# Block means by short products with the values standing, one load for the first value rows, and load costs by run length, in an attention and two-layer kernel

## The chip, the cores and the metric

The kernel runs on one core of a Trainium2 chip. The metric is the device time of one execution in microseconds (us). An execution is timed as a whole; the profile shows the span from the first to the last instruction on the core, which is a little shorter.

## What is computed

Local attention with block summaries, then two gated feed-forward stages, all in 32-bit floats:

```python
# B, H, S, D = 2, 8, 768, 64; block 32, window 16, nb = 24 blocks
k_sum = k.reshape(B, H, nb, block, D).max(axis=3)
v_sum = v.reshape(B, H, nb, block, D).mean(axis=3)
scores_l = scale * (q @ k.T), masked to |i - j| < window
scores_s = scale * (q @ k_sum.T) + log(block)
a = softmax over [scores_l, scores_s]
x = a @ concat([v, v_sum])              # 1536 tokens x 512
x = (silu(x @ w_gate) * (x @ w_val)) @ w_out        # 512 -> 1536 -> 512
out = (h * tanh(softplus(h))) @ w_out2, h = x @ w_in2   # 512 -> 2048 -> 512
```

## The kernel before

Attention is cut into 24 units: batch b, a third tb of the tokens (256), and a pair p of heads, in the order b, tb, p. A unit loads its queries (`loads`, 128 KB, runs of 1 KB in memory) and its windows of values (`load_v`, 192 KB into `vext[p]`: 96 rows, four windows, 128 columns, so runs of 512 bytes). `scores` makes the products of queries and keys (line 420), the scaled and masked scores with their minimum on VectorE (line 441), the exponentials on ScalarE (458) and the normalisation (483 on VectorE or 493 on ScalarE). `transposes` turns the weights (507) and copies them back; `values` makes the products with the values (523); its result is split into a high and a low part, `xh` by a copy on ScalarE (line 268) and `xl` by a subtraction on VectorE (line 282).

Each row of `vext[p]` below the 96 window rows holds the 24 block means. For the first batch they are made by `means_first`: six loads of 256 KB, six products on TensorE (line 342) in which a constant matrix of 128x120 stands and a tile of 128 tokens x 512 columns moves, summed in one bank, and then four copies on ScalarE into `vext[p]`. For the second batch `means_second` does the same when unit 6 is set up: six loads into `pacc`, six such products into one bank, one copy of 24x512 to `vsm`, from where `do_vext` spreads them by DMA.

The feed-forward stages work with numbers split in two fp32r parts, three products for one. Weights come as 512 KB tiles of 4 KB runs into four `raw` slots; each is put together by `words32` (lines 627 on ScalarE, 634, 643 and 652 on VectorE) and split into `wsl` (268 on ScalarE, 282 on VectorE). The first products that use them are those of `hidden` (line 722); the later stages are lines 773, 822 and 1005.

The order of the work is made by a planner in the program itself (`Program.order`). Every step is registered with an engine, a cost in ns, what it reads and writes, and for some a time at which it is wanted; the planner then lets the engines run by these costs and at each moment gives an engine, among the steps that are ready, the one whose latest allowed start is earliest. What comes out is a fixed order for each engine, which the chip follows whether or not its times are those of the planner. The transfers are all on the queue of SyncE. Their cost is `c_dma`; a transfer starts when the ones ahead have used up the planner's DMA time, and lands 1750 ns after its own share. `FIRST_LOADS` names the transfers that go first, in this order. Where TensorE has nothing to do by the planner's times, ahead of the first product of line 773, the planner puts filling products on a constant tile (line 256), in number 0.8 times the gap over 430 ns, and four at the start.

Of the kernel before, what the change touches and what calls it, by code (L numbers as in the profile page):

```python
# [17 lines left out]
P = 128  # L18
B, H, S, D = 2, 8, 768, 64
BLOCK, WINDOW = 32, 16  # L20
NB = S // BLOCK
SP = WINDOW + S + WINDOW
TQ = 64
NTILE = S // TQ
WIN = TQ + 2 * WINDOW
KC = WIN + NB
CCOLS = 3 * KC + P + KC + NB - P // BLOCK
NPAIR = H // 2
NT = B * S
DM = H * D  # L30
# [23 lines left out]
NORM_I, NORM_J = 4, 16  # L54


FIRST_LOADS = "k0 q0 c k1 q1 k2 q2 k3 q3 m0 m1 m2 m3 m4 m5 w0 w1 t0 w2 t1 w3 t2".split()

FILL_FIRST, FILL = 4, 0.8
EARLY, MEANS, NQ = 40e3, 25e3, 4  # L60
# [125 lines left out]
    return 100 + 2.35 * n  # L186


def c_dma(nbytes):
    return nbytes / 290.0  # L190


@with_exitstack
def tile_kernel(
# [14 lines left out]
    nc = tc.nc  # L209
# [7 lines left out]
    cst = sb.tile([P, CCOLS], F32, name="cst")  # L217
# [21 lines left out]
        for p in range(NPAIR)  # L239
    ]  # L240
    vx, qq = att[0:KC, 2 * KX :], att[:, 2 * KX + NPAIR * 512 :]
    vext = [vx[:, p * 512 : (p + 1) * 512].rearrange("p (n d) -> p n d", d=P) for p in range(NPAIR)]
    qraw = [qq[:, i * HALF : (i + 1) * HALF] for i in range(NQ)]
    qc = [
        qq[:, (NQ + i) * HALF : (NQ + i + 1) * HALF].rearrange("p (n q) -> p n q", q=TQ) for i in range(3)
# [7 lines left out]
    op = pg.add  # L253
# [3 lines left out]
    SC, PT, T1 = (0, 1, 2), (3, 4), (5, 6, 7)  # L257


    def dma(dst, src, nbytes, r=(), w=(), name=None, **more):  # L260
        if name in FIRST_LOADS:
            more["want"] = (FIRST_LOADS.index(name) - 100) * 500.0
        op("SP", c_dma(nbytes), lambda: nc.sync.dma_start(out=dst, in_=src), r=r, w=w, **more)

    def copy(dst, src, n, psum, r, w, scale=1.0, eng="ACT"):

# [23 lines left out]
    def att_bank(i):  # L290
        banks_used["n"] += 1
        ring = (2, 3, 6, 7, 4, 5) if i < 4 else (2, 3, 6, 7)
        return ring[banks_used["n"] % len(ring)]

    def do_k(b, p):
        ke, key = kext[p], ("kext", p)
        src = kt[b, p]
        if b == 0:

            stage = pacc[p // 2].rearrange("p m f -> p (m f)")[:, (p % 2) * 1024 : (p % 2) * 1024 + SP]  # L300
            sk = [("pacc", p // 2, m) for m in (2 * (p % 2), 2 * (p % 2) + 1)]
            dma(stage, src, P * SP * 4, w=sk, name=f"k{p}")
            win = bass.AP(stage.tensor, stage.offset, [stage.ap[0], [TQ, NTILE], [1, WIN]])
            copy(ke[:, :, 0:WIN], win, NTILE * WIN, False, sk, [key], eng=KE[p])
        else:
            win = bass.AP(src.tensor, src.offset, [[SP, P], [TQ, NTILE], [1, WIN]])
            dma(ke[:, :, 0:WIN], win, P * NTILE * WIN * 8, w=[key])
        ks = ksm[p % 2]
        op(
            "DVE",  # L310
            c_dve(S),
            lambda: nc.vector.tensor_reduce(
                out=ks.rearrange("p (t n) -> p t n", n=TQ // BLOCK),
                in_=ke[:, :, WINDOW : WINDOW + TQ].rearrange("p t (n r) -> p t n r", r=BLOCK),
                axis=AX.X,
                op=ALU.max,
            ),
            r=[key],
            w=[("ksm", p % 2)],
        )  # L320
        copy(
            ke[:, :, WIN:KC],
            ks.unsqueeze(1).to_broadcast([P, NTILE, NB]),
            NTILE * NB,
            False,
            [("ksm", p % 2)],
            [key],
            eng="POOL" if b else "DVE",
        )

    def means(b, bufs, bk):

        nt = S // P
        for t in range(nt):
            buf, key = bufs[t % len(bufs)]
            src = vt[b, WINDOW + t * P : WINDOW + (t + 1) * P, :]
            dma(buf, src, P * 2048, w=[key], name=f"m{b * nt + t}", rel=b * MEANS)
            at = NB - P // BLOCK - t * (P // BLOCK)
            op(
                "PE",  # L340
                860,
                lambda t=t, at=at, buf=buf: nc.tensor.matmul(  # L342
                    bank[bk][0:KC, :], mean[:, at : at + KC], buf, start=(t == 0), stop=(t == nt - 1)
                ),
                r=[key, "cst"],
                w=[("bank", bk)],
            )
# [21 lines left out]
    vsm, kvsm = pacc[1][WIN:KC, 3, :], ("pacc", 1, 3)  # L369

    def means_second():
        bk = att_bank(NPAIR)
        means(1, [(pacc[m // 4][:, m % 4, :], ("pacc", m // 4, m % 4)) for m in range(7)], bk)
        copy(vsm, bank[bk][WIN:KC, :], 512, True, [("bank", bk)], [kvsm])

    def do_vext(p):
        dma(
# [7 lines left out]
    def loads(i):  # L385
        b, tb, p = units[i]
        raw_q = qraw[i % NQ]
        dma(raw_q, qt[b, tb, p].rearrange("j d q -> (j d) q"), P * 1024, w=[("qraw", i % NQ)], name=f"q{i}")
        copy(
            qc[i % 3],  # L390
            raw_q.rearrange("d (q n) -> d n q", n=4),
            HALF,
            False,
            [("qraw", i % NQ)],
            [("qc", i % 3)],
            eng=QE[i] if i < NPAIR else "POOL",
        )

    def load_v(i):
        b, tb, p = units[i]  # L400
        src = vt[b, tb * HALF :, p * P : (p + 1) * P]
        win = bass.AP(src.tensor, src.offset, [[DM, WIN], [TQ * DM, 4], [1, P]])
        dma(vext[p][0:WIN, :, :], win, WIN * 2048, w=[("vext", p)], name=f"w{i}")

    def scores(i):

# [702 lines left out]
```

## Time and profile before

| | us |
|---|---|
| median of 3 runs | 630.26 (629.48 to 630.62) |
| the profiled execution | 629.81 |
| its span on the core | 627.8 |
| TensorE busy in the span | 616.9 |
| VectorE busy | 443.5 |
| ScalarE busy | 300.9 |
| GpSimd busy | 16.3 |

The span and the busy times come from the profiled execution; 2.0 us of its time lie outside the span. Busy time of TensorE is a union of its products' durations and does not say that each of them was at full rate, nor that each was needed: the filling products count too. The attention units run from 0 to some 125 us, overlapped with the first feed-forward stage from 26 us on.

### The profile page before, as it was taken

To read this page: it belongs to the slowest core of one execution; us is meant where nothing else is said; L and a number is where in the kernel's file an instruction comes from. 1 tells how busy PE (TensorE), PEld (TensorE's weight loads), DVE (VectorE), ACT (ScalarE), POOL (GpSimd) and SP (SyncE) were. 2 spreads that over 40 slices of the span, in tenths; PEclk is the share of its full clock that TensorE was granted. 3 is DMA by queue.
4 is the path that set the end of the run, shared out by engine and by line. 5 is a ranking of instruction groups with operands and counts; after the bars stand their busy time and mean duration, and the time that the engine had idled before them with its cause. 6 is when DMAs were issued, how large, how long until landed. Compare 5 with 4: busy or idle time off the path is not lost.

```text
span 627.8 us, 10576 instructions
## 1 busy us (share of the span) xinstructions
PE 616.9 (98%) x4020; PEld 530.6 (85%) x4020; DVE 443.5 (71%) x1075; ACT 300.9 (48%) x700; POOL 16.3 (3%) x29
## 2 busy tenths in 40 slices
PE   8999999999999999999999999999999999999997
PEld 5668989888888888888888888898989898989895
DVE  6898679665843884662665999689738985896553
ACT  5889998643512451331332545555443643362321
POOL 0021211000000000000000000000000000000000
PEclk9999999999999999999999999999999999999999
DMA  9985684012400350030200121213300340010111
GB/s 291 341 219 142 172 277 149 14 68 68 138 30 2 130 171 1 22 113 1 67 1 1 68 101 34 68 68 98 104 1 20 116 134 1 15 54 1 67 68 67
DMA packets 33713, 54.99 MB, mean 88 GB/s; under 512 B 8576, under 2 KB 21248, under 8 KB 33664
## 3 DMA queue, kind: packets, MB, share of 16 engines
q1 hardware_dynamic: 33664, 54.33, 27.9%
q8 instruction: 31, 0.51, 0.4%
q14 instruction: 18, 0.15, 0.1%
HBM read 50.98 MB, written 3.15 MB: 86 GB/s over the span
## 4 chain that ended last, share of the span: by engine, by line
PE 90%; ACT 4%; DMA 2%; DVE 2%; issue 1%; DVEq 0%; ACTq 0%; SPq 0%
PE bank L822 33%; PE bank L722 30%; PE bank L1005 19%; PE bank L773 3%; PE bank L420 2%; PE bank L523 2%; PE bank L507 1%; DMA raw<-in_w_val_dram 1%; ACT att_tmp L458 1%; PE bank L342 1%; ACT att_tmp L493 1%; DMA raw<-in_w_out_dram 1%; ACT cvs L627 1%; PE bank L256 1%; ACT att_tmp L268 1%
## 5 line engine op out<-in xcount | busy, mean ns | idle before, releaser
L722 PE MATMUL bank<-xh,wsl 128*128 128x512 f32 (+1 forms) x672 | 203.9, 363 | 0.9 <-DVE tmps L972 0.4
L722 PEld LDWEIGHTS bank<-xh,wsl 128*128 128x128 f32 x672 | 123.7, 188 | 22.4 <-DVE tmps L962 1.5
L822 PE MATMUL bank<-wsl,gt 128*128 128x512 f32 x576 | 135.5, 390 | 0.0
L822 PEld LDWEIGHTS bank<-wsl,gt 128*128 128x128 f32 x576 | 106.5, 188 | 21.0
L722 PE MATMUL bank<-xl,wsl 128*128 128x512 f32 (+1 forms) x336 | 120.4, 358 | 0.0
L822 PE MATMUL bank<-gt,wsl 128*128 128x512 f32 x360 | 91.3, 389 | 0.0
L1005 PE MATMUL bank<-xh,wsl 128*128 128x256 f32 x384 | 80.7, 283 | 1.1 <-ACT tmps L268 1.1
L822 PEld LDWEIGHTS bank<-gt,wsl 128*128 128x128 f32 x360 | 67.4, 188 | 13.9
L282 DVE TENSOR_TENSOR tmps<-tmps,bank 128x256 f32<-128x256 f32 x132 | 53.0, 416 | 33.9 <-PE bank L1005 31.9
L268 ACT ACTIVATE wsl<-cva 128x512 fp32r<-128x512 f32 (+1 forms) x84 | 50.5, 608 | 50.0 <-DVE cva L652 20.5
L722 PEld LDWEIGHTS bank<-xl,wsl 128*128 128x128 f32 x336 | 63.3, 188 | 9.4 <-issue 0.2
L962 DVE SCALAR_TENSOR_TENSOR tmps<-tmps,bank 128x512 f32<-128x512 f32 (+1 forms) x42 | 25.3, 603 | 61.8 <-ACT tmps L955 61.7
L1005 PEld LDWEIGHTS bank<-xh,wsl 128*128 128x128 f32 x384 | 64.9, 191 | 2.3 <-ACT tmps L268 1.3
L282 DVE TENSOR_TENSOR gt<-tmps,gt 128x512 fp32r<-128x512 f32 (+1 forms) x78 | 50.2, 645 | 21.7 <-ACT gt L268 17.4
L268 ACT ACTIVATE gt<-tmps 128x512 fp32r<-128x512 f32 (+1 forms) x77 | 45.4, 593 | 40.4 <-DVE tmps L972 39.1
L955 ACT ACTIVATE tmps<-bank 128x512 f32<-128x512 f32 (+1 forms) x42 | 22.5, 535 | 85.6 <-PE bank L722 85.5
L282 DVE TENSOR_TENSOR wsl<-cva,wsl 128x512 fp32r<-128x512 f32 (+1 forms) x84 | 55.1, 661 | 6.0 <-ACT wsl L268 6.0
L1005 PE MATMUL bank<-xl,wsl 128*128 128x256 f32 x192 | 54.3, 283 | 0.0
L1005 PE MATMUL bank<-att_late,wsl 128*128 128x256 f32 x320 | 49.3, 283 | 0.0
L627 ACT ACTIVATE cvs<-raw 128x512 f32<-128x512 f32 x68 | 44.8, 666 | 8.5 <-DVE cva L652 7.7
L652 DVE SCALAR_TENSOR_TENSOR cva<-cvs,cva 128x512 uint32<-128x512 uint32 x68 | 47.0, 692 | 0.5
L643 DVE SCALAR_TENSOR_TENSOR cva<-cvs,cva 128x512 uint32<-128x512 uint32 x68 | 46.0, 684 | 1.8 <-ACT cvs L627 0.6
(83 smaller groups left out, 687.2 us busy)
## 6 DMA issues: line engine op xcount, KB each, us to landing
raw<-in_w_out_dram SPq DMA_DIRECT2D x28, 512.0 KB, 3.7
raw<-in_w_in_dram SPq DMA_DIRECT2D x16, 512.0 KB, 3.6
raw<-in_w_gate_dram SPq DMA_DIRECT2D x12, 512.0 KB, 4.3
raw<-in_w_val_dram SPq DMA_DIRECT2D x12, 512.0 KB, 3.7
att<-in_vt_dram SPq DMA_DIRECT2D x24, 192.0 KB, 4.5
att<-in_qt_dram SPq DMA_DIRECT2D x24, 128.0 KB, 3.4
out_dram<-pacc SPq DMA_DIRECT2D x8, 256.0 KB, 2.1
pacc<-in_kt_dram SPq DMA_DIRECT2D x4, 400.0 KB, 6.0
```

What stands on the lines that cost most here:

```text
L268: cost, fn = c_act(n, psum), lambda: nc.scalar.activation(out=dst, in_=src, func=AF.Copy, scale=scale)
L282: op(eng, c_dve(n), lambda: nc.vector.tensor_tensor(out=dst, in0=a, in1=b, op=alu), r=r, w=w)
L420: nc.tensor.matmul(parts_[2 * j + n // 2][q, :], qb[d, n, :], ke[d, 4 * tb + n, :], start=True, stop=True)
L627: lambda: nc.scalar.activation(out=f32(q), in_=f32(high), func=AF.Copy, scale=2.0**-112),
L643: lambda: nc.vector.scalar_tensor_tensor(out=a, in0=q, scalar=3, in1=a, op0=ALU.logical_shift_left, op1=ALU.bitwise_or),
L652: lambda: nc.vector.scalar_tensor_tensor(out=a, in0=q, scalar=0x80000000, in1=a, op0=ALU.bitwise_and, op1=ALU.bitwise_or),
L722: nc.tensor.matmul(ps, a, x, start=(kk == 0 and m == 0), stop=(kk == KD - 1 and m == 2))
L773: nc.tensor.matmul(bank[bk][:, col : col + HALF], w[:, a, mm], gg[:, x, 0:sz], start=(n in starts and both == 1 and q == 0 and m % 2 == 0) ...
L822: nc.tensor.matmul(bank[m], lhs, rhs, start=(n in starts and both == 1 and q == 0), stop=(n in ends and both == 0),)
L955: lambda: nc.scalar.activation(out=t, in_=gate, func=AF.Tanh, scale=0.5),
L962: lambda: nc.vector.scalar_tensor_tensor(out=t, in0=t, scalar=1.0, in1=gate, op0=ALU.add, op1=ALU.mult),
L1005: nc.tensor.matmul(bank[bk][:, 0:HALF], w, x()[:, kk, :], start=(kk == 0 and m == 0), stop=(kk == 1 and m == 2),)
```

## The change

Three edits. The means of the second batch are made with the value tile standing and four constant columns moving: 24 products of 128x128 by 128x4 in place of six of 128x120 by 128x512, whose results (128 x 96) are copied by ScalarE into a tile that GpSimd has set to zero, turned back by four transposes on TensorE, and copied to `vsm` as before. The value windows of units 0 to 3 come in one load of 96 rows x 4 windows x 2 KB in place of four loads with runs of 512 bytes; for this `vext` is laid out window by window, so that the four pairs lie side by side. And the planner's cost of a load goes by the length of its runs: 390 bytes a ns from 2 KB, 300 from 1 KB, 215 below, in place of 290 for all; the key windows of the second batch are also counted at 4 bytes a number in place of 8.

```diff
-FIRST_LOADS = "k0 q0 c k1 q1 k2 q2 k3 q3 m0 m1 m2 m3 m4 m5 w0 w1 t0 w2 t1 w3 t2".split()
+FIRST_LOADS = "k0 q0 c k1 q1 k2 q2 k3 q3 m0 m1 m2 m3 m4 m5 w0 t0 t1 t2".split()
-def c_dma(nbytes):
-    return nbytes / 290.0
+def c_dma(nbytes, run=4096):
+    return nbytes / (390.0 if run >= 2048 else 300.0 if run >= 1024 else 215.0)
-    vext = [vx[:, p * 512 : (p + 1) * 512].rearrange("p (n d) -> p n d", d=P) for p in range(NPAIR)]
+    vext = [vx[:, 0:2048].rearrange("k (n p d) -> k p n d", p=NPAIR, d=P)[:, p] for p in range(NPAIR)]
-            dma(ke[:, :, 0:WIN], win, P * NTILE * WIN * 8, w=[key])
+            dma(ke[:, :, 0:WIN], win, P * NTILE * WIN * 4, w=[key], run=4 * WIN)
     def means_second():
-        bk = att_bank(NPAIR)
-        means(1, [(pacc[m // 4][:, m % 4, :], ("pacc", m // 4, m % 4)) for m in range(7)], bk)
-        copy(vsm, bank[bk][WIN:KC, :], 512, True, [("bank", bk)], [kvsm])
+        nt, nb = S // P, P // BLOCK
+        bk, bt = att_bank(NPAIR), att_bank(NPAIR)
+        sums = pacc[1][:, 2, 0 : NPAIR * KC].rearrange("p (a c) -> p a c", c=KC)
+        ks = ("pacc", 1, 2)
+        op("POOL", 300, lambda: nc.gpsimd.memset(pacc[1][:, 2, 0 : NPAIR * KC], 0.0), w=[ks])
+        blocks = mean[:, KC - nb : KC]
+        for t in range(nt):
+            buf, key = pacc[t // 4][:, t % 4, :], ("pacc", t // 4, t % 4)
+            src = vt[1, WINDOW + t * P : WINDOW + (t + 1) * P, :]
+            dma(buf, src, P * 2048, w=[key], rel=MEANS)
+            def products(t=t, buf=buf):
+                for p in range(NPAIR):
+                    at = p * NB + t * nb
+                    nc.tensor.matmul(
+                        bank[bk][:, at : at + nb], buf[:, p * P : (p + 1) * P], blocks, start=True, stop=True
+                    )
+            op("PE", 480, products, r=[key, "cst"], w=[("bank", bk)])
+        copy(
+            sums[:, :, WIN:KC],
+            bank[bk][:, 0 : NPAIR * NB].rearrange("p (a c) -> p a c", c=NB),
+            NPAIR * NB, True, [("bank", bk)], [ks],
+        )
+        def turn():
+            for p in range(NPAIR):
+                nc.tensor.transpose(bank[bt][0:KC, p * P : (p + 1) * P], sums[:, p, :], ident)
+        op("PE", 4 * 109, turn, r=[ks, "cst"], w=[("bank", bt)])
+        copy(vsm, bank[bt][WIN:KC, :], 512, True, [("bank", bt)], [kvsm])
     def loads(i):
-        dma(raw_q, ..., P * 1024, w=[("qraw", i % NQ)], name=f"q{i}")
+        dma(raw_q, ..., P * 1024, w=[("qraw", i % NQ)], name=f"q{i}", run=1024)
     def load_v(i):
         b, tb, p = units[i]
+        if i < NPAIR:
+            if i == 0:
+                win = bass.AP(vt.tensor, vt.offset, [[DM, WIN], [TQ * DM, 4], [1, DM]])
+                dst = vx[0:WIN, 0:2048].rearrange("k (n d) -> k n d", d=DM)
+                dma(dst, win, WIN * 8192, w=[("vext", h) for h in range(NPAIR)], name="w0")
+            return
-        dma(vext[p][0:WIN, :, :], win, WIN * 2048, w=[("vext", p)], name=f"w{i}")
+        dma(vext[p][0:WIN, :, :], win, WIN * 2048, w=[("vext", p)], run=512)
```

## Rows read from the trace of the kernel before

**Rows 1.** The page, busy time and share of the span by engine.
```profile
PE 616.9 (98%) x4020; PEld 530.6 (85%) x4020; DVE 443.5 (71%) x1075; ACT 300.9 (48%) x700; POOL 16.3 (3%) x29
```
**Rows 2.** Busy us in stretches of 10 us; then granted clock, DMA share, GB/s.
```profile
20.00:30.00 10.00, 8.62 (x101) 6.46 (x101) 8.90 (x30) 8.76 (x25) 1.48 (x2) 1.00 1.05 362
30.00:40.00 10.00, 9.65 (x70) 5.82 (x66) 9.38 (x30) 8.14 (x25) 1.77 (x2) 1.00 1.10 295
40.00:50.00 10.00, 9.46 (x117) 8.14 (x116) 9.89 (x37) 9.57 (x31) 2.39 (x3) 1.00 0.55 149
50.00:60.00 10.00, 9.55 (x123) 8.71 (x122) 7.96 (x31) 9.80 (x39) 1.61 (x3) 1.00 0.50 128
```
**Rows 3.** DMA, 10 to 24 us in 40 slices of 0.35 us: GB/s.
```profile
GB/s 392 404 421 392 386 421 380 394 366 348 214 212 200 195 274 236 168 262 316 312 319 249 211 258 260 288 265 345 294 225 237 269 259 306 307 389 389 416 395 348
```
**Rows 4.** The chain that ended last: start us, us, what.
```profile
12.01 2.58 PE bank L342 x6
15.36 2.78 PE bank L342 x6
...
20.49 0.39 ACT xh L268
20.87 0.57 ACT cvs L627
...
48.40 1.25 ACT att_tmp L493 x4
...
51.46 0.69 PE bank L523 x16
...
54.23 0.44 PE bank L507 x4
...
56.20 0.61 PE bank L523 x16
...
397.63 5.03 PE bank L1005 x42
```
**Rows 5.** VectorE in order of time: start us, us; in brackets idle before it.
```profile
17.48 0.17 DVE L471 TENSOR_SCALAR st<-st 128x4 f32<-128x4 f32 x1 [1.08 <-ACT att_tmp L458]
...
18.92 0.43 DVE L634 TENSOR_SCALAR cva<-raw 128x512 uint32<-128x512 uint32 x1 [0.17 <-DMA raw<-in_w_gate_dram]
20.91 0.42 DVE L282 TENSOR_TENSOR xl<-bank,xh 128x256 fp32r<-128x256 f32 x1 [1.56 <-ACT xh L268]
21.47 0.69 DVE L643 SCALAR_TENSOR_TENSOR cva<-cvs,cva 128x512 uint32<-128x512 uint32 x1
...
28.09 0.41 DVE L634 TENSOR_SCALAR cva<-raw 128x512 uint32<-128x512 uint32 x1
```
**Rows 6.** SyncE's issues; landing of the one at 11.09, then of all to 60 us.
```profile
11.09 0.35 SPq L263 DMA_DIRECT2D raw<-in_w_gate_dram  x1
...
14.10 0.35 SPq L263 DMA_DIRECT2D raw<-in_w_out_dram  x1
...
DMA to landing us min/median/max: 7.8/7.8/7.8
...
DMA to landing us min/median/max: 2.3/6.2/9.6
```
**Rows 7.** TensorE in order of time, the second batch's means begin.
```profile
30.37 1.98 PE L342 MATMUL bank<-pacc,cst 128*120 128x512 f32 x4
```
**Rows 8.** Groups by line: count | busy us, mean ns of one | idle before them.
```profile
L342 PEld LDWEIGHTS bank<-pacc,cst 128*120 128x120 f32 x12 | 2.0, 182 | 1.7 <-issue 1.6
L523 PEld LDWEIGHTS bank<-att_tmp,att 120*64 120x64 f32 x384 | 13.1, 137 | 6.2 <-ACT att_tmp L268 2.6 <-ACT att L268 0.9 <-ACT att_tmp L458 0.4
L268 ACT ACTIVATE att_tmp<-bank 120x512 f32<-120x512 f32 x24 | 14.1, 589 | 3.9 <-PE bank L507 3.9
L268 ACT ACTIVATE xh<-bank 128x256 fp32r<-128x256 f32 x24 | 9.0, 373 | 2.1 <-PE bank L523 1.8
L255 POOL MEMSET warm<- 128x256 f32 x1 | 0.3, 312 | 0.3 <-POOLq L1097 0.3
```

More of the change, by code (lines that the diff above doesn't have):

```diff
@@ L257, in tile_kernel, with dma @@
     SC, PT, T1 = (0, 1, 2), (3, 4), (5, 6, 7)
-    def dma(dst, src, nbytes, r=(), w=(), name=None, **more):
+    def dma(dst, src, nbytes, r=(), w=(), name=None, run=4096, **more):
         if name in FIRST_LOADS:
             more["want"] = (FIRST_LOADS.index(name) - 100) * 500.0
-        op("SP", c_dma(nbytes), lambda: nc.sync.dma_start(out=dst, in_=src), r=r, w=w, **more)
+        op("SP", c_dma(nbytes, run), lambda: nc.sync.dma_start(out=dst, in_=src), r=r, w=w, **more)
     def copy(dst, src, n, psum, r, w, scale=1.0, eng="ACT"):
@@ L371, in means_second @@
     def means_second():
-        bk = att_bank(NPAIR)
-        means(1, [(pacc[m // 4][:, m % 4, :], ("pacc", m // 4, m % 4)) for m in range(7)], bk)
-        copy(vsm, bank[bk][WIN:KC, :], 512, True, [("bank", bk)], [kvsm])
+        nt, nb = S // P, P // BLOCK
[18 more added lines that the diff above has]
+            bank[bk][:, 0 : NPAIR * NB].rearrange("p (a c) -> p a c", c=NB),
+            NPAIR * NB,
+            True,
+            [("bank", bk)],
+            [ks],
+        )
[4 more added lines that the diff above has]
+        copy(vsm, bank[bt][WIN:KC, :], 512, True, [("bank", bt)], [kvsm])
     def do_vext(p):
@@ L387, in loads @@
         raw_q = qraw[i % NQ]
-        dma(raw_q, qt[b, tb, p].rearrange("j d q -> (j d) q"), P * 1024, w=[("qraw", i % NQ)], name=f"q{i}")
+        dma(raw_q, qt[b, tb, p].rearrange("j d q -> (j d) q"), P * 1024, w=[("qraw", i % NQ)], name=f"q{i}", run=1024)
         copy(
```

## The prediction

> **What bounds the kernel now.** I read four views, each to answer the question that the one before left. The busy shares come first: TensorE is busy 98% of the span [rows 1], so whatever does not change what TensorE does late in the kernel has to show up as TensorE starting its dense part earlier or doing less in it. The stretches of 10 us come second: between 20 and 50 us TensorE is not the only full engine; VectorE is busy 28.2 of 30 us there (8.90, 9.38, 9.89) and ScalarE 26.5 [rows 2]. All three edits bear on the first 50 us, so the question is who is late there. The chain of waits is third: it runs over TensorE until 18.14 us (the first batch's means end there, 15.36 + 2.78), then over ScalarE's copies and conversions, VectorE's conversions of weights, ScalarE's normalisations and exponentials, and only from 51.46 us over TensorE without a break [rows 4]. The second batch's means begin at 30.37 us [rows 7], inside the part in which the chain is not on TensorE. VectorE's own timeline is fourth: it stands idle 1.08 us before 17.48, 0.17 before 18.92 and 1.56 before 20.91, 2.8 us in all [rows 5], and from 20.91 on it has hardly a gap until 50. So the start is a stream of conversions and softmax steps on VectorE and ScalarE, fed by loads; what makes this stream begin sooner moves the whole rest of the kernel, and what only relieves TensorE before 51 us need not.
>
> **Part 1, the first value rows as one load.** The loads from 10 us on run at 348 to 421 GB/s (390 on average) until 13.5 us, then at 168 to 345 for 25 slices of 0.35 us, and after 22.2 us again at 348 to 416 [rows 3]. The slow part is the stretch in which the value loads of 512-byte runs are mixed with the first weights. Its 25 slices add up to 6481, which over 0.35 us each is 2.27 MB; at 390 GB/s these take 5.8 us and not 8.75. So the load saves at most 2.9 us of DMA time, if its 2 KB runs go as fast as the 2 KB runs of the means' loads before 13.5 us, and nothing if they do not. The Trainium skill ("DMA: Bandwidth & Descriptors", Specifications) gives 512 bytes as the size from which a transfer runs at line rate; by that rule 512-byte runs lose nothing, and this edit would be worth 0 and not 2.9 us. The slices disagree with it here.
>
> What does the saved DMA time buy? The first weight tile is issued at 11.09 and lands 7.8 us later at 18.89; VectorE takes it at 18.92 [rows 5, 6]. It now stands behind all four windows (786 KB) where it stood behind two (393 KB). At 390 GB/s the former take 2.0 us; at 215, the slow slices, the latter take 1.8; so this tile lands about when it did. The second and the third gain the most, up to 2.9 us; but the third, issued at 14.10 [rows 6], is taken by VectorE only at 28.09 [rows 5], 14 us later, while no load of the first 60 us took longer than 9.6 to land [rows 6]. So the loads are not what VectorE waits for after 20.91; the order is. That brings in part 3. The values of unit 0 now wait for the whole of the windows, not for a quarter: three quarters more, 590 KB, are 1.5 us at 390 GB/s. These windows are issued at about 10 us, ahead of the weight tile of 11.09, so they land ahead of its 18.89, while the values of unit 0 cannot start before the means' copies that follow 18.14. This cover is some 1 us deep; without it, the late part would fall on the values one for one. Three issues less on SyncE are off every path.
>
> **Part 2, the second batch's means.** Removed are six products, each two records of 0.43 us (2.58 over 6 [rows 4]): 12 x 0.43 = 5.2 us of TensorE. Added are 24 products of two records, each with a new standing tile of 128 columns and four moving columns, so 48 records. No row has this form. The lowest bound is the values' product, 0.61 us for 16 records or 0.038 us, with only 64 standing columns and halves of the array in parallel [rows 4]: 48 of them are 1.8 us. The highest is the record of line 1005 with a new 128-column tile each time, 5.03 over 42 = 0.120 us [rows 4]: 5.8 us. The transposes that come on top are four at 0.44 us together [rows 4]. The loads of standing tiles take 182 ns at 120 columns and 137 at 64 [rows 8], 45 ns for 56 columns, or 0.80 ns a column; if the loads can't overlap each other, 128 columns hold the array 0.103 us and 48 are 4.9 us. I take this, since it is the row nearest in kind: 4.9 + 0.44 = 5.4 against 5.2 us, no saving. The ends are a saving of 3.0 us (5.2 less 1.8 and 0.44) and a loss of 1.0 us (5.8 + 0.44 less 5.2). The Trainium skill ("TensorE: Matmul & The Clock Gate", LDWEIGHTS) gives a load as the columns over 1.2 in ns, whatever the rows; that is 107 ns here, an estimate of 5.1 us for the 48 and 5.6 with the transposes, and speaks against this edit as a saving. Where the planner has the work done is before 51.46 us, so each of these ends is first of all idle time of TensorE and is cut by the chain on VectorE and ScalarE. In 30 to 40 us TensorE is busy 9.65 of 10 us [rows 2], so not all of it is hidden; I put a tenth of the saving's end on the path, -0.3 us, and keep -2 and +0.5 for the range.
>
> On ScalarE a copy of 96 columns is added. Copies of 512 and 256 columns take 0.589 and 0.373 us [rows 8], 0.84 ns a column, so 96 take 0.24 us. ScalarE is busy 9.57 of 10 us in 40 to 50 us and on the chain there [rows 2, 4]: I count it in full, +0.24 us; behind it in ScalarE's order wait exponentials and weight copies. The zeroing on GpSimd covers 480 columns; 256 took 0.312 us [rows 8], so at most 0.6 us, on an engine busy 16.3 us of the whole span [rows 1]. Only query copies are queued behind it; 0.
>
> **Part 3, the planner's costs.** By the old costs the first loads, up to the third weight tile, add up to 22.1 us; by the new ones to 16.9 us (keys 4 x 1.05, queries 4 x 0.44, constants 0.82, means 6 x 0.67, windows 2.02, weights 3 x 1.34). With 1.75 us to land, the planner expected the first weight tile at 18.9 us, which is what the trace shows (18.89 [rows 6]); it will now expect it at 15.9. Two effects. ScalarE's first conversion stood behind the high part of unit 0's values (20.49, then 20.87 [rows 4]); expected earlier, it is put ahead of it and of the copies before that. Then VectorE's stream starts at about 19.4 to 20 and not 21.47 [rows 5], 1.5 to 2.1 us earlier, out of the 2.8 us in which it now idles. I take 1.6 us, and let it carry through to 51.46, since VectorE and ScalarE are both full from there on. Against it, the planner expects things up to 2 us before they come, which can put a waiting conversion ahead of a ready step; this is the rival below. The filling products change in number, but they stand where TensorE would idle.
>
> **The sum.** 629.81 us (span 627.8 and 2.0 around it) - 1.6 (stream) - 0.3 (TensorE) + 0.24 (ScalarE) = 628.15; I say 628.3, taking 0.15 off the gain for new gaps after 52 us, where TensorE has 0.45 us idle in 10 [rows 2]. The profiled execution stands 0.45 us under the median, so against the median this is -0.3%. A measurement of this kernel can tell about 0.2%, 1.26 us: faster means under 629.0, slower over 631.5.
>
> **The rivals.** *A larger gain*: the whole 2.9 us of DMA and 2 us of TensorE arrive at the end: 629.81 - 2.9 - 2 + 0.24 = 625.2. For it: TensorE's 9.65 of 10. Against it: VectorE has 2.8 us to give and is full afterwards. *Hidden*: the loads come sooner and nobody takes them sooner, since VectorE's 28.2 busy us of 30 decide; or the one load is no faster than the four. Then 629.81 + 0.24 and some change of order: 630.0. For it: the third tile waits in its slot until 28.09. *Slower*: the planner's optimism. It moves the third tile's landing up by 5.3 us (23.9 to 18.6 by its costs) and the real loads gain at most 2.9. If the conversions are put so far ahead that ScalarE or VectorE stand waiting for a tile with softmax steps behind it, up to 5.3 - 2.9 = 2.4 us are lost in a stream with no slack: 629.81 + 2.4 + 0.24 = 632.4. It decides if VectorE reaches its second or third tile earlier than the tile lands. For it: an engine's order is fixed. Against it: TensorE's own lag (the means end at 18.14) holds the stream back anyway.
>
> **How the numbers follow.** Forecast 0.44 (its own range 627.2 to 629.2), larger gain 0.12, hidden 0.25, slower 0.19. Faster: 0.42 of the forecast and 0.12, 0.54; same: 0.02, 0.22 of the hidden and 0.01, 0.25; slower: 0.18 and 0.03, 0.21. The range, 625.6 to 631.8, leaves out the far half of the larger gain and of the slower case, some 0.16 in all.
>
> **What would show it.** Right: the slow slices after 13.5 us gone, VectorE's line 643 starting before 20.5, its idle before that under 1.5 us, TensorE's unbroken part starting near 50. For part 2: 48 short records, their spacing read from the start of one group to the next. Wrong: VectorE or ScalarE idle with a DMA as releaser between 16 and 30 us; a start of the unbroken part at 51.5 or later; or a gap of TensorE after 52 us that the kernel before did not have.

## The result and the profile after

The changed kernel takes 636.45 us (median of six executions, 635.50 to 637.19) where the kernel before takes 629.76 on the same chip (628.54 to 630.62): 1.0102 times as long, with an interval of 1.0089 to 1.0115. It is slower by 6.7 us. The forecast was 628.3 us.

The page of the changed kernel has TensorE at the same 98% as [rows 1], and 5.7 us busier:

```profile
PE 622.6 (98%) x4062; PEld 539.4 (85%) x4062; DVE 443.6 (70%) x1075; ACT 301.4 (47%) x701; POOL 17.3 (3%) x30
```

Where the time went is read first from the chain that ended last (start us, us, what), against [rows 4]:

```profile
33.47 1.03 PE bank L389 x8
...
35.07 3.15 PE bank L389 x24
38.22 0.85 PE bank L763 x3
39.06 3.21 PE bank L389 x16
...
59.46 0.69 PE bank L564 x16
...
405.13 5.03 PE bank L1046 x42
```

The unbroken part of TensorE begins at 59.46 us and no longer at 51.46: 8.0 us later. The same step far behind it, 397.63 before, is now at 405.13, 7.5 us later. So the loss is there by 60 us and nothing is added after it. And the chain now runs over the new short products (line 389); the six products whose place they take (line 342, from 30.37 us on [rows 7]) were not among its rows.

The second view is the busy time in stretches of 10 us (columns as in [rows 2]; the number after the five busy times is the granted clock of TensorE):

```profile
20.00:30.00 10.00, 8.12 (x99) 5.64 (x88) 9.57 (x42) 9.86 (x30) 2.84 (x4) 1.00 1.07 326
30.00:40.00 10.00, 8.98 (x85) 8.09 (x84) 8.77 (x24) 6.13 (x19) 1.45 (x2) 0.87 0.96 313
40.00:50.00 10.00, 10.00 (x77) 9.60 (x78) 4.38 (x17) 5.03 (x17) 0.46 (x1) 0.62 0.34 93
```

From 40 to 50 us VectorE falls from 9.89 busy us [rows 2] to 4.38 and ScalarE from 9.57 to 5.03, while TensorE is busy all 10 us, does 77 records instead of 117, and is granted 0.62 of its clock. In stretches of 2 us of the same view:

```profile
34.00:36.00 2.00, 2.00 (x30) 1.82 (x30) 2.00 (x6) 1.00 (x2) 0.74 (x1) 1.00 1.09 347
36.00:38.00 2.00, 2.00 (x17) 2.00 (x16) 2.00 (x6) 1.29 (x5) 0.00 (x0) 0.83 0.98 390
38.00:40.00 2.00, 2.00 (x12) 2.00 (x11) 0.77 (x3) 0.90 (x2) 0.00 (x0) 0.50 1.02 329
40.00:42.00 2.00, 2.00 (x11) 2.00 (x12) 1.58 (x8) 0.04 (x1) 0.00 (x0) 0.50 1.07 273
42.00:44.00 2.00, 2.00 (x11) 2.00 (x11) 0.00 (x0) 1.00 (x3) 0.00 (x0) 0.50 0.56 176
44.00:46.00 2.00, 2.00 (x12) 2.00 (x11) 1.60 (x3) 1.12 (x5) 0.00 (x0) 0.50 0.01 5
46.00:48.00 2.00, 2.00 (x12) 1.96 (x11) 0.04 (x1) 1.31 (x5) 0.00 (x0) 0.61 0.00 0
48.00:50.00 2.00, 2.00 (x39) 1.65 (x38) 1.17 (x6) 1.56 (x6) 0.46 (x1) 1.00 0.04 13
```

TensorE stands at 0.50, the 1.2 GHz level, for 10.2 us (four whole stretches, and by their shares 0.7 us of the stretch at 0.83 and 1.6 of the one at 0.61). It is never idle in this time, nor in the 2 us before it: busy 2.00 of 2.00, on every row. (From 30 to 32 us it had been busy 1.13 of 2 us, so some idle time does lie ahead; e5, below, is busy 1.40 there and keeps its clock.) What it did before the clock fell is on its timeline:

```profile
33.47 1.03 PE L389 MATMUL bank<-cst,pacc 128*128 128x4 f32 x8
34.43 0.64 PE L461 MATMUL bank<-kx,att 64*64 64x120 f32 x16
35.00 3.22 PE L389 MATMUL bank<-cst,pacc 128*128 128x4 f32 x24
...
38.86 3.41 PE L389 MATMUL bank<-cst,pacc 128*128 128x4 f32 x16
```

From 33.47 on these are the records with four moving columns, with 16 score products between the first groups. While the clock is full they follow each other at about 0.12 us; the last 16 take 3.21 us (chain above), 0.20 us each. Who waits for this is on ScalarE's timeline (in brackets the idle time ahead and what ended it):

```profile
39.10 0.38 ACT L996 ACTIVATE tmps<-bank 128x256 f32<-128x256 f32 x1 [1.81 <-PE bank L763]
...
42.37 0.25 ACT L269 ACTIVATE pacc<-bank 128x96 f32<-128x96 f32 x1 [2.33 <-PE bank L389]
...
46.67 0.59 ACT L269 ACTIVATE pacc<-bank 24x512 f32<-24x512 f32 x1 [1.55 <-PE bank L405]
```

The same stretch that was bound by VectorE and ScalarE before (the chain's rows from 32 us on) is bound by TensorE now. The Trainium skill ("Perfetto Trace Analysis", opening note) says that matmul busy time is a poor measure of how near a kernel is to its limit. The rows here agree, though for another reason than the Trainium skill gives there, which is that matmuls are pipelined: the busiest stretch of TensorE, 40 to 50 us, is the one in which it does least, 77 records, because its clock is low.

The start of the kernel also changed. VectorE's timeline, against [rows 5]:

```profile
15.93 0.86 DVE L524 TENSOR_SCALAR att_tmp<-att_tmp,st 128x120 f32<-128x120 f32 x4
19.91 0.43 DVE L675 TENSOR_SCALAR cva<-raw 128x512 uint32<-128x512 uint32 x1 [3.13 <-DMA raw<-in_w_gate_dram]
...
21.23 0.28 DVE L482 CUSTOM_DVE_ANT_0 att_tmp<-bank,cst 128x120 f32<-128x120 f32 x1
```

VectorE stands 3.13 us before the first weight tile and does the scores of unit 2 (the row of 21.23) only behind it; before, it had done them by the time the tile came. And the DMA slices of 0.35 us from 10 to 24 us, against [rows 3]:

```profile
GB/s 413 386 427 398 398 416 392 369 392 375 316 228 205 257 234 234 246 228 199 246 275 222 246 328 386 398 433 398 421 410 386 427 342 448 380 433 383 348 389 418
```

The slow part is still there, at some 230 GB/s, with runs of 2 KB where they were 512 bytes; it is 13 slices long, 4.5 us.

### The profile page after: what moved, and what is told of

It is laid out like the page before. It is cut to its first block, busy times and chain, and to the rows that moved or that the text cites. A ratio compares the mean times of both kernels' runs of the same rounds, so it can differ in the third digit from the quotient of the medians.

```text
span 635.3 us, 10658 instructions
## 1 busy us (share of the span) xinstructions
PE 622.6 (98%) x4062; PEld 539.4 (85%) x4062; DVE 443.6 (70%) x1075; ACT 301.4 (47%) x701; POOL 17.3 (3%) x30
## 4 chain that ended last, share of the span: by engine, by line
PE 91%; DMA 4%; DVE 2%; ACT 1%; SPq 1%; issue 0%; POOL 0%; DVEq 0%; POOLq 0%; ACTq 0%
PE bank L863 33%; PE bank L763 31%; PE bank L1046 18%; PE bank L814 3%; DMA att<-in_qt_dram 2%; PE bank L564 2%; PE bank L461 2%; DMA raw<-in_w_gate_dram 1%; PE bank L548 1%; PE bank L389 1%; SPq L264 1%; DMA pacc<-in_vt_dram 0%; DVE pacc L894 0%; DVE cva L684 0%; DVE kx L283 0%
## 5 line engine op out<-in xcount | busy, mean ns | idle before, releaser
L283 DVE TENSOR_TENSOR gt<-tmps,gt 128x512 fp32r<-128x512 f32 (+1 forms) x78 | 50.4, 649 | 22.8 <-ACT gt L269 18.4
```

The costliest lines, as they stand in the source:

```text
L283: op(eng, c_dve(n), lambda: nc.vector.tensor_tensor(out=dst, in0=a, in1=b, op=alu), r=r, w=w)
```

## The experiments

Two theories stood after the comparison. *Clock*: the short products lower TensorE's clock, and this is most of the 6.7 us. *Start*: the window load and above all the planner's new costs spoil the order of the first 20 us, and the clock falls because everything is late. Fourteen kernels were run; the kernel before took 629.76 to 629.84 us beside them.

| kernel | us | ratio, interval |
|---|---|---|
| e1: before, with the short products | 636.32 | 1.0100 [1.0068, 1.0132] |
| e4: changed kernel, with the old means | 632.33 | 1.0035 [1.0024, 1.0047] |
| e5: changed kernel, 120 moving columns | 632.21 | 1.0039 [1.0027, 1.0051] |
| e7: before, with the products of e5 | 631.08 | 1.0035 [1.0022, 1.0048] |
| e3: before, new costs only | 631.10 | 1.0014 [1.0001, 1.0028] |
| e2: before, one window load only | 630.32 | 1.0012 [1.0003, 1.0021] |
| e6: e2, loaded as 64 and 32 rows | 629.96 | 1.0003 [0.9990, 1.0016] |
| e10: e2, loaded as 128 rows | 630.09 | 0.9999 [0.9988, 1.0010] |
| e8: e4, window load costed at 215 bytes/ns | 632.85 | 1.0048 [1.0033, 1.0063] |
| e9: e4, three means held back | 633.06 | 1.0049 [1.0036, 1.0062] |
| e14: e4, new costs for weights only | 628.99 | 0.9989 [0.9980, 0.9998] |
| e15: e4, old costs for weights only | 631.90 | 1.0035 [1.0022, 1.0048] |
| e16: e14, windows in 128 rows | 628.88 | 0.9991 [0.9980, 1.0002] |
| e17: changed kernel with the costs of e14 | 636.50 | 1.0083 [1.0058, 1.0109] |

### One part at a time

**e1.** The kernel before with `means_second` of the changed kernel and nothing else.

```diff
...
-        means(1, [(pacc[m // 4][:, m % 4, :], ("pacc", m // 4, m % 4)) for m in range(7)], bk)
...
+            def products(t=t, buf=buf):
+                for p in range(NPAIR):
+                    at = p * NB + t * nb
+                    nc.tensor.matmul(bank[bk][:, at : at + nb], buf[:, p * P : (p + 1) * P], blocks, ...)
...
+                nc.tensor.transpose(bank[bt][0:KC, p * P : (p + 1) * P], sums[:, p, :], ident)
...
```

> The kernel before with the short products alone; loads and costs are the old ones. Theory clock (the short products lower TensorE's granted clock and most of the loss is the time at half clock): the granted clock falls below 1.00 somewhere between 30 and 50 us and the time is 633 to 635.5, that is 3.5 to 6 us over before. Theory order (the loss comes from the planner's new costs, which let steps wait for loads): 629.5 to 630.5 and a clock of 1.00 throughout.

It took 636.32 us, as long as the whole change. Its stretches of 2 us show the same picture 2 us earlier (by the shares of the rows the clock falls at 35.4 us and not 37.3):

```profile
34.00:36.00 2.00, 2.00 (x17) 2.00 (x17) 2.00 (x7) 1.42 (x5) 0.00 (x0) 0.84 1.11 305
36.00:38.00 2.00, 2.00 (x12) 2.00 (x10) 1.89 (x9) 1.09 (x5) 0.80 (x1) 0.50 1.10 221
...
42.00:44.00 2.00, 2.00 (x10) 2.00 (x11) 1.02 (x3) 1.56 (x6) 0.00 (x0) 0.50 0.14 50
44.00:46.00 2.00, 2.00 (x13) 2.00 (x12) 0.33 (x1) 0.40 (x1) 0.00 (x0) 0.60 0.00 0
```

The start is that of the kernel before here (VectorE takes the first weight tile at 19.03 us, against 18.92), and the clock falls all the same, with TensorE busy 2.00 of 2.00 us from 32 us on. So a late start is not what lowers it.

**e2.** The one window load alone, with the old cost of 290 bytes/ns.

```diff
+                win = bass.AP(vt.tensor, vt.offset, [[DM, WIN], [TQ * DM, 4], [1, DM]])
+                dst = vx[0:WIN, 0:2048].rearrange("k (n d) -> k n d", d=DM)
+                dma(dst, win, WIN * 8192, w=[("vext", h) for h in range(NPAIR)], name="w0")
...
```

> The kernel before with the one load for the first four value windows alone; the planner's costs and the means are the old ones. If the 2 KB runs carry the windows at the rate of the means' loads (390 GB/s): no slices under 300 GB/s after 13 us and 627.5 to 629.5. If the rate hangs on the 96 rows and not on the length of the runs: some 4 us near 230 GB/s as in the changed kernel, and 629.5 to 630.5, no difference. If holding the first weight tile behind all four windows is what costs: 630.5 to 632.

630.32 us: the load brings nothing, and perhaps costs half a microsecond.

**e3.** The new `c_dma` alone, with the run lengths that it is given and the 4 bytes a number for the key windows, and with the four loads of before.

```diff
-def c_dma(nbytes):
-    return nbytes / 290.0
+def c_dma(nbytes, run=4096):
+    return nbytes / (390.0 if run >= 2048 else 300.0 if run >= 1024 else 215.0)
...
```

> The kernel before with the new costs of loads alone (four value loads, long products). Theory clock: 630 to 632, clock 1.00. Theory order: 633 to 637, with VectorE idle for more than 2 us ahead of its first conversion.

631.10 us: by the medians the costs lose 1.3 us, by the interval 0.1 to 1.8, where they were to win 1.6.

**e4.** The changed kernel with the old `means_second`; load and costs stay.

> The changed kernel with the second batch's means made as before (long products), the one load and the new costs kept. Theory clock: 630 to 632, clock 1.00 throughout; what is left over before is the wait of the first conversions for the first weight tile, 1 to 2 us. Theory order: 635 to 637, hardly below the changed kernel.

632.33 us. Load and costs together lose 2.6 us by themselves. The two losses, 6.5 (e1) and 2.6, would make 9; the change costs 6.7. They don't add so: the short products cost 6.5 us in the order of the kernel before, but 4.1 in that of the changed kernel (632.33 to 636.45).

### The clock

**e5.** The same 24 standing tiles in the changed kernel, but with 120 moving columns instead of 4. The tiles are taken in the reverse order, so that each product writes over what the product before it left outside its four columns; the same block means are left in the end, by more work.

```diff
-        blocks = mean[:, KC - nb : KC]
+        wide = mean[:, 0:KC]
...
-                        bank[bk][:, at : at + nb], buf[:, p * P : (p + 1) * P], blocks, start=True, stop=True
+                        bank[bk][:, at + nb - KC : at + nb], buf[:, (NPAIR - 1 - p) * P : (NPAIR - p) * P], wide, start=True, stop=True
...
```

> The changed kernel in its own order, with the same 24 standing value tiles, but 120 moving columns in each product in place of four (116 of them zeros, overwritten by the products that follow). TensorE has more to do: 48 records of about 0.10 us. Theory clock: the clock stays at 1.00 and the time falls to 630.5 to 632.5 although the products are longer. Theory order: 636 to 638. If the standing loads and not the shortness of the products bring the clock down: clock below 1.00 again and 636 to 638.

632.21 us, 4.2 less than the changed kernel. Its stretches of 10 us and its TensorE timeline:

```profile
30.00:40.00 10.00, 9.40 (x100) 8.66 (x99) 9.71 (x31) 6.42 (x20) 1.03 (x1) 1.00 1.03 325
40.00:50.00 10.00, 9.75 (x117) 8.23 (x116) 8.46 (x25) 9.84 (x33) 0.99 (x2) 1.00 0.32 93
```

```profile
34.52 2.94 PE L389 MATMUL bank<-cst,pacc 128*128 128x120 f32 x24
...
37.67 1.94 PE L389 MATMUL bank<-cst,pacc 128*128 128x120 f32 x16
```

The clock stays at 1.00, the 2.4 GHz level, and VectorE is back at 8.46 us. That holds beyond the profiled execution: the mean clock of e5's ten executions is 0.996 to 1.000, that of the changed kernel's six 0.991 to 0.994. A record takes 2.94 / 24 = 0.12 us with 120 moving columns, as much as with four at the full clock. So the narrow product saves no time at all, and the wide one keeps the clock. It also bounds what the low clock costs: products of `hidden` follow each other at 1.43 / 12 = 0.119 us in the chain of e5 and at 2.56 / 12 = 0.213 in that of the changed kernel at 0.50, 1.79 times as long; the 10.2 us at 0.50 are then 5.7 us of work, 4.5 lost. The measured 4.2 is near that. Beside the old means in the same order (e4, 632.33) the wide form costs nothing.

**e7.** The same in the kernel before: the wide products alone, old load and costs.

> The kernel before with the new means in their wide form alone (24 standing value tiles, 120 moving columns; old loads and costs), beside the same kernel with four moving columns, which took 636.3. If the moving columns decide the clock: clock 0.996 to 1.00, 629.5 to 631. If the standing loads or the new order at unit 6 cost by themselves: 632 or more.

631.08 us by the median, with a mean clock of 1.000 in the profiled execution: 5.2 us less than e1, which differs only in the width and, with it, in the order of the tiles. Four of the seven executions took 631.0, the other three, with a mean clock of 0.996 or 0.997, 632.7 to 633.0; even these are 3 us under e1. What is left over the kernel before is 1.3 us by the medians and 1.4 to 3.0 by the interval. The new form at the full clock comes to 1.25: 48 records at 0.12 and transposes of 0.44 are 6.2 us where 5.2 were, and the copy of 0.25 us on ScalarE. That this sum is the cause is not shown; in the order of the changed kernel the same form costs nothing (e5 beside e4). *Clock* holds: of the 6.5 us of e1, some 5.2 are the clock and 1.3 the form.

### The window load

**e6 and e10.** The one load of e2 in other numbers of rows: as a load of 64 rows and one of 32, and as one load of 128 rows, of which the last 32 are read by nobody. The order on every engine is that of e2 in e10.

```diff
-                win = bass.AP(vt.tensor, vt.offset, [[DM, WIN], [TQ * DM, 4], [1, DM]])
+                win = bass.AP(vt.tensor, vt.offset, [[DM, P], [TQ * DM, 4], [1, DM]])
-                dst = vx[0:WIN, 0:2048].rearrange("k (n d) -> k n d", d=DM)
+                dst = att[:, 2 * KX : 2 * KX + 2048].rearrange("k (n d) -> k n d", d=DM)
```

> As the kernel with the one load alone, but the 96 rows are loaded in two pieces, 64 rows and 32 rows, with the same 2 KB runs and the same bytes. If the slow rate comes from how 96 rows are shared out over the DMA engines: the slices near 230 GB/s become 300 to 390, the windows land 1 to 1.5 us sooner, 628 to 629.5. If it comes from the source (windows that overlap by a third) or from the run length: the slices stay near 230 GB/s and the time equals that of the one load.

> As the kernel with the one load alone (630.3), every engine in the same order, but the load fills 128 rows in place of 96 (1.05 MB in place of 0.79; the 32 rows more are overwritten by the means or not used). If the rate hangs on the number of rows: slices near 390 GB/s in place of 230, the windows land about 0.8 us sooner although a third more is moved, and the time is 629 to 630. If it hangs on the overlapping source or on 2 KB runs: slices stay near 230, the windows land 1.1 us later, 630.5 to 631.5.

The DMA slices from 10 to 24 us, first of e2, then of e6, then of e10:

```profile
GB/s 418 404 398 421 398 404 410 380 398 375 240 211 205 217 211 187 211 228 269 269 258 252 240 252 240 304 398 386 386 445 433 398 363 372 392 386 433 377 296 138
```

```profile
GB/s 398 392 416 398 410 398 410 398 392 392 164 135 146 135 140 158 211 217 228 211 252 234 275 258 199 246 433 421 386 386 421 421 445 363 375 389 395 445 363 375
```

```profile
GB/s 411 414 402 389 392 392 351 363 375 310 222 222 357 410 398 375 374 398 451 404 410 421 451 375 433 421 421 398 392 378 293 342 152 336 389 287 193 47 99 29
```

With the same runs of 2 KB, and the loads behind it mixed in toward the end, the load into 96 rows (e2) goes at 187 to 304 GB/s for sixteen slices from the eleventh on, the one into 64 rows (e6) begins there with six at 135 to 164, slower than either expectation had it, and the one into 128 rows (e10) has three at 222 to 310 from the tenth on and then eighteen at 357 to 451. In the three the DMA engines were busy 0.8, 0.5 and 0.5 of the time, since SyncE issued the load 1.1 us later than in e2 (11.47 against 10.38 us); e16, below, has no such gap and moves 375 to 456 GB/s from the eleventh to the 28th slice. In the slow slices of e2 and e6 they were busy 0.8 and more, so the few rows do not leave engines idle. The number of rows sets the rate, not the run. The Trainium skill ("SBUF — State Buffer", Door 1: The DMA port swizzle) says that the first 64 rows reach only half of the ports by which transfers enter, and the next 64 the other half. By it, as an estimate, 64 rows go at half the rate, 195 of 390, and 96 rows, bounded by their first 64, at three quarters, 293. The slices agree in the order and lie lower in both cases. The time, though, did not follow: 629.96 and 630.09 us. The slow stretch is off the path in this order, as the rival *hidden* had it.

### The start

**e8.** e4 with the window load costed as it goes (215 bytes/ns).

```diff
-                dma(dst, win, WIN * 8192, w=[("vext", h) for h in range(NPAIR)], name="w0")
+                dma(dst, win, WIN * 8192, w=[("vext", h) for h in range(NPAIR)], name="w0", run=512)
```

> The changed kernel with the old means, and the one window load counted in the planner at 215 bytes a ns in place of 390, near what it was seen to run at (230 GB/s): the planner then expects the first weight tile 1.6 us later. Theory optimism (the planner puts the first conversion ahead of attention steps because it expects the tile too early): VectorE's wait of 3 us for the first tile shrinks below 1.5 us and the time falls from 632.3 to 630 to 631.3. Theory position (the tile simply comes late behind all windows): 632 to 633 still.

632.85 us, no gain by the median of four: the six means still stood ahead of the scores of unit 2, and VectorE waited 3.82 us for those instead of for the tile. The one execution with a mean clock of 1.000 took 631.44, so a gain of 1 us is not excluded.

**e9.** e4 with the last three products of the first batch's means held back in the planner.

```diff
+                rel=15000.0 if b == 0 and t >= 3 else 0.0,
```

> The changed kernel with the old means, and in the planner the last three products of the first batch's means held back until 15 us, so that the transposes of unit 0 and the scores of unit 2 come ahead of them as in the kernel before (the new costs had put all six means first). Theory order of the start (the 2.5 us that loads and costs lose together come from unit 2's scores standing behind all means and unit 0's values): scores of unit 2 before 16 us and not at 20.4, VectorE's idle stretch of 3.6 us gone, 630 to 631. Theory late tile (what matters is when the first weight tile lands): 632 to 633 still.

633.06 us. The scores of unit 2 came back to where they were, but VectorE's timeline shows the next victim:

```profile
17.03 0.08 DVE L450 DVE_READ_ACCUMULATOR2_ANT st<- 128x1 f32 x1
19.89 0.43 DVE L643 TENSOR_SCALAR cva<-raw 128x512 uint32<-128x512 uint32 x1 [2.77 <-DMA raw<-in_w_gate_dram]
20.23 0.16 DVE L480 TENSOR_SCALAR st<-st 128x4 f32<-128x4 f32 x1
```

The conversion of the first tile waits 2.77 us with the normalisation of unit 2 (line 480) behind it. Moving one step did not help while the planner took every load for landed too early. But the time is not the price of the order alone: in this execution TensorE is granted 0.50 of its clock from 24 to 28 us, without any short product.

**e14 and e15.** e4 with half of the new costs each: new for the weights and old (290) for the first keys, queries, constants, means and windows; and the reverse.

```diff
+        cost = nbytes / 290.0 if name and name[0] in "kqcmw" else c_dma(nbytes, run)   # e14
+        cost = nbytes / 290.0 if name and name[0] == "t" else c_dma(nbytes, run)       # e15
```

> The one window load and the old means; of the new costs only those of the weights' loads (4 KB runs, 390 bytes/ns) and of the later loads, while the first keys, queries, constants, means and windows keep the old cost of 290 bytes/ns, so that TensorE's order up to the scores of unit 2 is that of the kernel before (transposes, three means, scores, three means). Theory (what costs 2.5 us is that the early loads' new prices move all six means ahead of the scores of unit 2): 630.0 to 630.8 us, the unbroken part of TensorE from 51.5 to 52.5 us. Rival (the weights' new price alone, with conversions ahead of softmax steps, costs it): 631.8 to 632.8 us.

> The mirror image: the one window load and the old means; the new costs for the first keys, queries, constants, means and windows, the old cost of 290 bytes/ns for the weights' loads. All six means stand ahead of the scores of unit 2. Theory (early loads' prices): 632.0 to 632.8 us, with VectorE waiting 2 to 4 us for the scores of unit 2 around 20 us. Rival (weights' price): 630.0 to 630.8 us.

628.99 and 631.90 us, 2.9 apart. VectorE in e14 and then in e15:

```profile
18.17 0.86 DVE L492 TENSOR_SCALAR att_tmp<-att_tmp,st 128x120 f32<-128x120 f32 x4
19.87 0.43 DVE L643 TENSOR_SCALAR cva<-raw 128x512 uint32<-128x512 uint32 x1 [0.84 <-DMA raw<-in_w_gate_dram]
```

```profile
15.81 0.86 DVE L492 TENSOR_SCALAR att_tmp<-att_tmp,st 128x120 f32<-128x120 f32 x4
20.51 0.43 DVE L643 TENSOR_SCALAR cva<-raw 128x512 uint32<-128x512 uint32 x1 [3.85 <-DMA raw<-in_w_gate_dram]
20.89 0.28 DVE L450 CUSTOM_DVE_ANT_0 att_tmp<-bank,cst 128x120 f32<-128x120 f32 x1
```

In e14 VectorE fills the time up to the tile with the scores and the normalisation of unit 2 and waits 0.84 us; in e15 it waits 3.85 and does that work, some 2 us (four score steps at 0.2 us and 1.2 us of normalisation), behind the tile. So the loss of the start is in the prices of the early loads (e4 and e14, 3.3 us apart, differ in these and besides only in the prices of the later queries and of the second batch's means). With them the planner puts all six means ahead of the scores of unit 2; that this step of the order is what costs is not shown, since e9, which undid it by itself, was no faster (though its clock had fallen as well). The lower price of the weights is not harmful: e14, lower than either expectation had it, is the fastest kernel but for e16, 0.8 us under the kernel before; its interval ends just below 1, and the gain is less than the 0.2% that counts as a difference here.

**e16 and e17.** e14 with the windows in 128 rows; and the changed kernel, short products and all, with the costs of e14.

> The version with the old means, one window load and only the weights' loads at the new price (628.99 us), with the windows loaded in 128 rows instead of 96 (the 32 more rows are not read by anyone); the order on every engine is the same. Theory (in this order VectorE waits 0.84 us for the first weight tile before 19.87, so the load is now on the path): 0.3 to 0.8 us less, 628.2 to 628.7. Rival (loads are hidden here too, as they were with the old prices): 628.8 to 629.2 us.

> The changed kernel with its short products, but with the old price of 290 bytes/ns for the first keys, queries, constants, first-batch means and windows, so that three means, the scores of unit 2 and three means follow each other as before. Theory (two losses that add: the order of the start about 2.5 to 3.3 us, the short products with their clock 5 to 6.5 us): 634.0 to 635.5 us, granted clock 0.50 for 8 us or more between 30 and 50 us. Rival (one is the cause of the other: the clock falls because the start is late): 629.0 to 631 us with no stretch at 0.50.

628.88 us for e16: the rate of the load doesn't matter here either, although VectorE had waited 0.84 us in e14 for the tile behind it. For e17 the median is 636.50, but its six executions lie in two groups: four at 636.3 to 637.0, with a mean clock of 0.988 or 0.989, and two at 633.0, with 0.992. The profiled execution is one of the four (stretches of 2 us):

```profile
10.00:12.00 2.00, 1.07 (x20) 0.91 (x21) 1.93 (x11) 2.00 (x5) 0.00 (x0) 0.96 1.05 405
12.00:14.00 2.00, 2.00 (x5) 0.94 (x4) 2.00 (x8) 2.00 (x7) 0.50 (x1) 0.50 1.07 369
14.00:16.00 2.00, 2.00 (x5) 0.67 (x3) 1.79 (x9) 1.53 (x6) 0.00 (x0) 0.69 1.06 227
...
34.00:36.00 2.00, 2.00 (x30) 1.82 (x29) 2.00 (x6) 1.09 (x5) 0.00 (x0) 0.93 1.05 315
36.00:38.00 2.00, 2.00 (x11) 2.00 (x11) 2.00 (x7) 1.77 (x5) 0.64 (x1) 0.50 0.81 244
```

The clock falls at 36 us as in e1, though the order of the start has been put right; so *start* is not the cause of that. But in this execution it had fallen once before, from 12 us on, where no short product stands. The three upper rows lose 1.7 us of clock, 0.003 of the span, which is about the difference between the mean clocks of the two groups. The two executions at 633.0 have no trace; that their start ran at the full clock is worked out from this and not shown.

Taken so, the two groups say what the median hides. Without the early fall, putting the start right is worth 3.5 us in the changed kernel (636.45 to 633.0; its profiled execution has no early fall either), as it is with the old means (e4 to e14, 3.3), and the short products cost 4.0 us over e14 as they cost 4.1 over e4. In these two executions, then, the losses of the start and of the short products add. My sum (634.0 to 635.5) was too high because it took for the products what they cost in the order of the kernel before. With the early fall e17 takes 3.3 to 4.0 us more, which is more than the 1.7 us of clock; the rest is open.

The same early fall stands in the profiled executions of e2, e3, e4, e8 and e16 (0.50 to 0.56 from 12 to 14 us). In e16 it can be priced: the three executions with a mean clock of 0.996 or 0.997 took 630.4 to 631.0 us, the other nine 628.3 to 629.9. In e4 nothing hangs on it: its two executions at 1.000 took 632.4 and 633.2, the others 631.3 to 633.0.

## Why the prediction was wrong

**The step that failed is the lower and upper bound of part 2.** I bounded 48 new records by rows at the full clock, 0.038 to 0.120 us, and so the edit by a gain of 3.0 and a loss of 1.0 us. The clock was 1.00 on every row of [rows 2], and I took it for a constant; no bound and no rival had a term for it. The upper end was right for the records at the full clock (0.12), the value taken, 0.103, was low: the form costs 1.3 us in the order of the kernel before (e7), and nothing in that of the changed kernel (e5 beside e4), where I had 0.2 + 0.24. The missing term is 4.2 us in the order of the changed kernel (e5) and 5.2 in that of the kernel before (e7 against e1). It falls on the path, as the chain over line 389 shows, because TensorE, with 9.65 of 10 us busy in 30 to 40 [rows 2], had no room to run at half speed; I had read the same number as "not all of it is hidden" and had kept only half a microsecond for a loss.

**Part 1 failed on its cause, and the rival held.** I put the slow slices [rows 3] down to runs of 512 bytes. The number of rows does it (e2, e6, e10), so that the one load was no faster per byte. The first tile, said to land about when it did, landed 1.0 us later (19.89 against 18.89 [rows 6]), because the windows ahead of it took some 4.5 us and not 2.0. Against the 512 bytes of the Trainium skill ("DMA: Bandwidth & Descriptors", Specifications) I had trusted the slices; its verdict, no gain from the longer runs, came true (e2). That the time hangs little on the load, the rival *hidden*, is what e10 and e16 show. The cover for the values of unit 0 was too thin as well: in the changed kernel TensorE waits 0.90 us for the windows before 18.98.

**Part 3 had the sign wrong.** The forecast was 1.6 us earlier; alone the costs lose 1.3 (e3, 0.1 to 1.8 by the interval). The rival *slower* named the mechanism, a conversion that waits for its tile with softmax steps behind it, priced it at 2.4 us and gave the time as 632.4. Load and costs without the new means take 632.33 (e4). So this rival was right as to load and costs in its mechanism, with a chance of 0.19 that was too low. That its number fits so closely is luck: it took off 2.9 us that the loads were to gain and did not, and its condition was the second or third tile, while VectorE waits for the first (3.13 us). Its evidence was in the sum that I used as a gain: the planner was to expect the tile at 15.9, three us before it came, and VectorE already idled there [rows 5]. I had it gain from the earlier order without asking what would be put behind the waiting conversion.

**The chain was read with a gap.** Between 20.87 and 48.40 us [rows 4] I named only ScalarE and VectorE. Two loads of weights stand there too, 10.8 us:

```profile
21.46 6.37 DMA raw<-in_w_val_dram
27.91 4.38 DMA raw<-in_w_out_dram
```

So "the loads are not what VectorE waits for after 20.91" does not follow from the chain. In the changed kernel 19.7 of the 22.8 us from 10.68 to 33.45 are loads:

```profile
10.68 9.21 DMA raw<-in_w_gate_dram
...
20.98 7.50 DMA att<-in_qt_dram
...
30.51 2.95 DMA pacc<-in_vt_dram
```

The chains of e1 and e14 have no load between 10 and 62 us, so near ties decide whether one stands there; what these loads are worth no run settles.

**What was right:** the effect was there before 60 us and was carried through (8.0 us there, 7.5 far behind), GpSimd's zeroing (0.50 us at 12.96) held nothing up, the copy took 0.25 us against 0.24, and the unbroken part of TensorE was the mark to look at. By its own list ("a start of the unbroken part at 51.5 or later", "VectorE or ScalarE idle with a DMA as releaser between 16 and 30 us") the trace said at once that the forecast had failed.

## What to carry to other kernels

Before narrowing the moving side of products that stand in dense work, ask what the clock of TensorE will do: a record with a new standing tile takes as long with 4 moving columns as with 120, and the row to look at is the granted clock, not the busy share. Each correction of a planner's prices moves the order, also where the new price is nearer the truth for one load; ask what ends up waiting with what behind it, and change the prices in halves (as in e14 and e15) before trusting them together. When two losses meet in one stretch, measure each alone and in the order in which it will stand, and look at the clock of every execution before trusting a median: that of e17 hid two groups 3.5 us apart and with them the gain of the better start.

## What the runs showed of the hardware

- TensorE can be busy 2.00 of 2.00 us on each row and yet be granted only 0.50 of its clock (changed kernel, 38 to 46 us; e1, 36 to 44): it fell after groups of records with 4 moving columns and was back at 1.00 behind products with 256 moving columns. With 120 moving columns in the places of the 4 it stayed at 1.00 there (profiled executions of e5 and e7). Why the 4 columns lower it no run shows.
- Short products are not the only way to the low level: the clock also stood at 0.50 from 12 to 14 us in e2, e3, e4, e16 and e17, and from 24 to 28 us in e9, with none near. TensorE had idled ahead of that (busy 1.07 of 2 us from 10 to 12 in e17; 1.26, 0.90 and 1.29 from 18 to 24 in e9), but the changed kernel idled as much (1.10 and 0.92 from 18 to 22) and kept 1.00.
- A record with a new 128-column standing tile in 32-bit floats follows the last at 0.12 us, with 4 or 120 moving columns. The Trainium skill ("TensorE: Matmul & The Clock Gate", LDWEIGHTS) gives a load as the columns over 1.2 in ns, whatever the rows, which is an estimate of 107 ns for 128 columns; the records show 0.12 us, a tenth above it.
- A load into 96 rows ran at about 230 GB/s (e2, and the changed kernel), into 64 at about 140 (the first six slices of e6), into 128 at about 390 (e10, e16), with the same runs of 2 KB.
